# Attention, then two feed-forward layers in float32r on one Trainium2 core: the first layer's token parts moved to other distances, modulo 512 bytes, from the weights

## The chip, the core and the metric

The kernel runs on one core of one Trainium2 chip. The metric is the time of one execution on the device in microseconds (us). The core has TensorE (PE) for matmuls, VectorE (DVE), ScalarE (ACT) and GpSimd (POOL) for elementwise work, and SyncE (SP), whose queue issues nearly all DMAs here.

## The reference

Attention with 4 batches, 8 heads, 576 tokens and 64 columns a head, then two feed-forward layers over the 2304 tokens.

```python
scores = scale * np.matmul(q, k.transpose(0, 1, 3, 2))      # causal, softmax -> a
local = np.matmul(a, v)
mem_out = mem_ret / mem_norm                                # phi(q) times M_prev, over phi(q) times z_prev
attn_out = g * mem_out + (1 - g) * local
...
h = x @ w_in                                                # (2304 x 512) @ (512 x 2048)
x = softplus(h) @ w_out                                     # (2304 x 2048) @ (2048 x 512)
...
a, b = x @ w_a, x @ w_b                                     # (2304 x 512) @ (512 x 1536)
out = (a * b) @ w_out2                                      # (2304 x 1536) @ (1536 x 512)
```

## The kernel before, in words

**Stages.** Attention takes 16 units (a batch and a pair of heads each). Then come `h` (below: the first layer, matmul line L875), its product with `w_out` (the second layer, L1019), `a` and `b` together (the third, L875 again), and the last product (L1019 again). The 2304 tokens go in three groups of 768.

**One product.** Each layer multiplies blocks of two by two by Strassen's scheme, so seven products, numbered 1 to 7, stand for eight. For each, the token side is a sum or difference of blocks; so is the weight side. Each operand is split into two float32r parts, high and low ("h" and "l"), and three matmuls (h times h, h times l, l times h) replace one float32 matmul. A first-layer unit (one of eight blocks of `w_in`, one token group) is 7 products of 6 matmuls, so 42 matmuls of 384 columns; the first layer has 24 units, 1008 matmuls. In every one of them the weights are 128 columns of float32r (512 bytes a partition), loaded anew, and the token part is the operand that streams.

**Where the token parts lie.** `right_parts` makes, for a group, the 14 token parts (7 products, h and l) of 768 words each. They lie one after the other in SBUF from word X0 = 14848, X1 = 25600 and X2 = 36352 for the three groups (a word is 4 bytes; `in_order` sets the steps of 1536 words per product). The weights of the first layer lie from WL = 4096 in three buffers of 3584 words. All these are multiples of 128 words, so every token part starts at the same place modulo 512 bytes as every 128-column slice of the weights. In attention, `kh` and `kl` (the operand that streams in the score matmuls, L517) are taken in turn from two buffers of 576 words, and `qh`, `ql` (the weights there) from two of 512 words: for even units k lies at 0 bytes modulo 512 from q, for odd units at 256 bytes (576 words is 4.5 times 128; from the place of `kh`, word 30080, which is 235 times 128). The memory operand `mz` (L555) has two buffers, 264 words apart, and is read in slices of 65 words.

**Who sets the order.** The kernel records every operation with its operands (`Plan.add`), finds what each depends on, gives each a cost, and a list scheduler (`order`) writes one fixed order for each engine; a semaphore wait stands for each dependence. Inside one buffer, dependences are found word by word (`cells`). Between two buffers that overlap in SBUF, everything is taken together (`beside`): whoever writes the one waits for all earlier uses of the other, to the last.

```python
for o in self.over.get(name, ()):
    for wrote, read in self.state[o].values():
        yield from (n for n, _ in wrote)
        if not reads:
            yield from (n for n, _ in read)
```

**What else lies there.** During attention, X1 and the words behind it hold `kr0`, `kr1` (from word 25600), `qr`, `qh` and so on. After the first layer's last units, `Wide` (the second layer) puts its own buffers over the token parts: weights `w5` (product 5) at words 32768 to 36864, `w6` at 43008 to 47104, token tiles `t0` at 23552, `t1` at 36864 to 39936, `t2` at 12288, `t3` at 39936 to 43008. `left` loads one product's weights (`w5lf` and so on) and splits them (ACT makes h, DVE makes l, in two halves each); `sums` makes a product's token sums on DVE (a tile in two halves, `t00` and `t01`); `parts` makes a slice's h (ACT) and l (DVE) into four buffers `gx0` to `gx3` in turn. One product of the second layer is four such slices, 12 matmuls each, so 48 matmuls; the order of the products is 1, 2, 5, 6, 7, 3, 4.

Of the kernel before, what the change touches and what calls it, by code (L numbers as in the profile page):

```python
# [10 lines left out]
F32R = mybir.dt.float32r  # L11
# [11 lines left out]
HALF = 384  # L23
GT = 2 * HALF
# [299 lines left out]
def tile_kernel(ctx: ExitStack, tc: tile.TileContext, qt, kt, vt, mz, be, w_in, w_out, w_a, w_b, w_2, out):  # L324
    nc = tc.nc
    plan = Plan(tc)
    V, A, G, PE, SP = (
        Engine(plan, n, e) for n, e in (("DVE", nc.vector), ("ACT", nc.scalar), ("POOL", nc.gpsimd), ("PE", nc.tensor), ("SP", nc.sync))
    )
# [18 lines left out]
    def kept(shape, name):  # L348
        return plan.track(nc.dram_tensor(name, shape, F32, kind="Internal").ap())
# [3 lines left out]
    xs = [kept([128, KT, GT], f"xs{i}") for i in range(NG)]  # L353
# [10 lines left out]
    def put(name, words, *at, dtype=F32):  # L364

        tag = name + "_" * (name in where)
        where[name] = [plan.buffer(f"{tag}{i}", words, a, dtype) for i, a in enumerate(at)], [0]
# [27 lines left out]
    RAW, WL, X0, X1, X2, SUMS = 0, 4096, 14848, 25600, 36352, 49664  # L395
    put("raw", 2048, RAW, RAW + 2048)
    early, late, spare = space(X1), space(X2), space(SUMS)
    more = space(WL + 7168)
    for n, words in (("kr", S), ("qr", 640), ("qh", 512), ("ql", 512), ("kh", S), ("kl", S), ("ph", 640)):
        at = [early(words), early(words)] + [more(words)] * (n in ("kr", "qr"))  # L400
# [387 lines left out]
            sub(e, w[:, n:m, 1], d[:, n:m], f(w[:, n:m, 0]))  # L788
        return lambda n, h, k: w[:, SLOT[n], h, 128 * k : 128 * k + 128]

    def right_parts(src, at, step=2, e=V, raws=()):

        x = {
            n: [plan.buffer(f"x{n}{h}", GT, a + GT * i, F32R).rearrange("p (k t) -> p k t", k=2) for i, h in enumerate("hl")]
            for n, a in at.items()
        }
        t = []
        for k in range(2):
            r = (raws[k] if k < len(raws) else take("raw"))[:, 0 : 2 * GT].rearrange("p (k t) -> p k t", k=2)
            SP.dma_start(out=r, in_=src[:, 2 * k : 2 * k + 2])  # L800
            t.append(r)
        (b11, b12), (b21, b22) = ((r[:, :, 0:HALF], r[:, :, HALF:GT]) for r in t)

        def parts(n, b):
            for k in range(0, 2, step):
                u = slice(k, k + step)
                rnd(A, x[n][0][:, u], b[:, u])
                sub(e, x[n][1][:, u], b[:, u], f(x[n][0][:, u]))

        parts(1, b11)  # L810
        sub(e, b11, b12, b11)
        parts(5, b11)
        sub(e, b11, b22, b11)
        parts(6, b11)
        parts(2, b21)
        sub(e, b12, b22, b12)
        parts(7, b12)
        parts(3, b22)
        sub(e, b21, b21, b11)
        parts(4, b21)  # L820
        return x
# [5 lines left out]
    def in_order(at):  # L827
        return {n: at + 1536 * i for i, n in enumerate((1, 5, 6, 2, 7, 3, 4))}
# [70 lines left out]


    plan.stream = 1
    put("s", HALF, *(50688 + HALF * i for i in range(12)))
    put("plain", 1024, 47104, 48128)
    put("more", 768, 49152, 49920)
    at_w = [WL, WL + 3584, WL + 7168]
    W1, X = {}, {}
    X_AT = [in_order(X0), in_order(X1), in_order(X2)]

    def unit1(u, g):
        def out(i, j, s, bank):  # L910
# [13 lines left out]
    def prepare1(what):  # L924
        kind, n = what[0], int(what[1:] or 0)
        if kind == "t":
            put("s", HALF, *(53760 + HALF * i for i in range(5)), *(47104 + HALF * i for i in range(6)))
            return
        if kind == "w":
            W1[n] = left_parts(w_in[n], at_w[n % 3], G if n in FIRST else V)  # L930
        elif kind == "x":
            raws = [plan.buffer("third", 2048, 47104)] if n == 2 else []
            X[n] = right_parts(xs[n], X_AT[n], 2 - (n == 0), G if n == 0 else V, raws)
        else:
            spill_out()

# [305 lines left out]
```

## Time and profile before

| what | value |
|---|---|
| time, median of 3 runs | 920.23 us (919.73, 920.23, 921.40) |
| span of the profiled execution, first to last instruction | 918.2 us |
| PE busy | 905.9 us, 99% of the span, 6556 matmuls |
| DVE busy | 786.6 us, 86% |
| ACT busy | 564.9 us, 62% |
| POOL busy | 100.4 us, 11% |
| DMA | 172.16 MB, 187 GB/s on average |

The profiled execution has no device time of its own on the page. Its span is the time from its first instruction to its last, and it is 2.0 us under the median of the runs; what lies around it (start and end of the program) makes the difference. A matmul's duration in the trace (334 ns) overlaps the next one's, so its price is read from the distance between starts.

### The profile page before, as it was taken

How to read it: one execution, taken by the hardware profiler on the slowest of the kernel's cores; microseconds unless marked ns; L12 is line 12 of the kernel's file. 1: busy time of each engine (PE TensorE's matmuls, PEld its weight loads, DVE VectorE, ACT ScalarE, POOL GpSimd, SP SyncE). 2: the span in 40 equal slices, each digit the busy share in tenths (PEclk: the TensorE clock that was granted, in tenths of full speed). 3: DMA queues.
4: the chain of work that ended last, by engine and by line, in shares of the span. 5: the costliest groups of instructions: out<-in, count | busy, mean ns of one | idle time of the engine just before them, and what ended most of it. 6: DMA issues, size and time to landing. Idle time of an engine off the chain costs nothing.

```text
span 918.2 us, 17626 instructions
## 1 busy us (share of the span) xinstructions
PE 905.9 (99%) x6556; PEld 868.2 (95%) x6556; DVE 786.6 (86%) x1487; ACT 564.9 (62%) x1124; POOL 100.4 (11%) x140
## 2 busy tenths in 40 slices
PE   6999999999999999999999999999999999999998
PEld 4777778899999999999999999999999999999998
DVE  6999999789999658988599999999899666988683
ACT  7999999677677576744456655444444344655442
POOL 6445667100000000000000000000000000000000
PEclk9999999999999999999999999999999999999999
DMA  7656654468889889672720445455656156672701
GB/s 231 192 157 184 191 155 127 135 237 273 287 305 303 290 296 374 218 246 80 225 75 23 161 149 181 161 167 179 215 185 220 48 185 186 227 248 88 215 26 52
DMA packets 84870, 172.16 MB, mean 187 GB/s; under 512 B 8352, under 2 KB 60976, under 8 KB 82096
## 3 DMA queue, kind: packets, MB, share of 16 engines
q1 hardware_dynamic: 84352, 170.71, 56.9%
q8 instruction: 51, 0.84, 0.4%
q10 hardware_dynamic: 432, 0.33, 0.1%
q14 instruction: 35, 0.29, 0.1%
HBM read 110.90 MB, written 60.11 MB: 186 GB/s over the span
## 4 chain that ended last, share of the span: by engine, by line
PE 98%; DVE 1%; DMA 0%; issue 0%; ACT 0%; SPq 0%; DVEq 0%
PE bank L875 48%; PE bank L1019 33%; PE bank L627 4%; PE bank L597 4%; PE bank L517 4%; PE bank L555 1%; PE bank L668 1%; PE bank L647 1%; PE bank L614 1%; PE bank L635 1%; DVE eTrue L527 0%; DMA kr<-kt 0%; PE bank L570 0%; PE bank L653 0%; PE bank L615 0%
## 5 line engine op out<-in xcount | busy, mean ns | idle before, releaser
L346 DVE TENSOR_TENSOR s<-bank,s 128x384 f32<-128x384 f32 x216 | 117.9, 552 | 40.8 <-PE bank L875 31.5
L853 ACT ACTIVATE s<-bank 128x384 f32<-128x384 f32 x72 | 35.0, 486 | 81.2 <-PE bank L875 52.0
L343 DVE TENSOR_TENSOR t<-t,t 128x1536 f32<-128x1536 f32 (+1 forms) x48 | 74.5, 1552 | 0.4
L875 PE MATMUL bank<-x1h,w 128*128 128x384 f32 x240 | 70.7, 335 | 0.0
L875 PE MATMUL bank<-x5h,w 128*128 128x384 f32 x240 | 70.6, 334 | 0.0
L875 PE MATMUL bank<-x3h,w 128*128 128x384 f32 x240 | 70.5, 334 | 0.0
L875 PE MATMUL bank<-x7h,w 128*128 128x384 f32 x240 | 70.5, 334 | 0.0
L875 PE MATMUL bank<-x6h,w 128*128 128x384 f32 x240 | 70.5, 334 | 0.0
L875 PE MATMUL bank<-x2h,w 128*128 128x384 f32 x240 | 70.5, 334 | 0.0
L875 PE MATMUL bank<-x4h,w 128*128 128x384 f32 x240 | 70.5, 334 | 0.0
L336 ACT ACTIVATE w<-wf 128x256 fp32r<-128x256 f32 (+1 forms) x100 | 50.1, 501 | 19.4 <-DVE w L343 14.7
L911 ACT ACTIVATE s<-s 128x384 f32<-128x384 f32 x72 | 37.5, 523 | 32.9 <-DVE s L346 32.5
L850 ACT ACTIVATE s<-bank 128x384 f32<-128x384 f32 x72 | 34.9, 485 | 32.1 <-PE bank L875 16.6
L336 ACT ACTIVATE gx1h<-t 128x768 fp32r<-128x768 f32 x37 | 31.3, 847 | 34.4 <-PE bank L1019 33.1
L336 ACT ACTIVATE gx2h<-t 128x768 fp32r<-128x768 f32 x37 | 31.4, 847 | 34.2 <-PE bank L1019 31.8
L343 DVE TENSOR_TENSOR w<-wf,w 128x256 fp32r<-128x256 f32 (+1 forms) x90 | 47.3, 525 | 3.7 <-ACT w L336 3.2
L336 ACT ACTIVATE gx0h<-t 128x768 fp32r<-128x768 f32 x37 | 31.3, 846 | 30.4 <-PE bank L1019 28.9
L759 ACT ACTIVATE raw<-raw 128x512 f32<-128x512 f32 (+1 forms) x54 | 43.2, 802 | 9.0 <-DVE raw L758 8.6
L343 DVE TENSOR_TENSOR gx1l<-t,gx1h 128x768 fp32r<-128x768 f32 x37 | 35.3, 954 | 13.5 <-ACT gx1h L336 13.3
L343 DVE TENSOR_TENSOR gx0l<-t,gx0h 128x768 fp32r<-128x768 f32 x37 | 35.3, 954 | 12.8 <-ACT gx0h L336 12.5
L856 ACT ACTIVATE s<-bank 128x384 f32<-128x384 f32 x72 | 35.3, 490 | 17.1 <-PE bank L875 12.9
L336 ACT ACTIVATE gx3h<-t 128x768 fp32r<-128x768 f32 x36 | 30.4, 845 | 24.1 <-PE bank L1019 24.0
(340 smaller groups left out, 2982.1 us busy)
## 6 DMA issues: line engine op xcount, KB each, us to landing
gs<-s SPq DMA_DIRECT2D x96, 192.0 KB
t<-gs SPq DMA_DIRECT2D x24, 768.0 KB
us<-s SPq DMA_DIRECT2D x72, 192.0 KB
t<-us SPq DMA_DIRECT2D x12, 768.0 KB
raw<-w_out SPq DMA_DIRECT2D x8, 1024.0 KB
raw<-w_in SPq DMA_DIRECT2D x12, 512.0 KB
raw<-w_a SPq DMA_DIRECT2D x12, 512.0 KB
raw<-w_b SPq DMA_DIRECT2D x12, 512.0 KB
```

The costliest lines, as they stand in the source:

```text
L336: A.activation(out=o, in_=i, func=AF.Copy)
L343: eng.tensor_tensor(out=o, in0=a, in1=b, op=ALU.subtract)
L346: eng.tensor_tensor(out=o, in0=a, in1=b, op=ALU.add)
L517: PE.matmul(out=s[:, j, at : at + L], lhsT=a[r, qc], rhs=b[r, 0:L], start=t == 0, stop=t == 2, skip_group_check=True,)
L597: PE.transpose(out=s[:, 128 * n : 128 * n + 128], in_=Es[i, j][:, 128 * k : 128 * k + 128], identity=ident)
L627: PE.matmul(out=self.po[both[j], 128 * k :], lhsT=self.vr[:, k, 64 * j : 64 * j + 64], rhs=a, start=False, stop=k == 3, skip_group_check=True,
L759: A.activation(out=f(high), in_=f(high), func=AF.Identity, scale=REBIAS)
L853: A.activation(out=self.s5, in_=bank["c"], func=AF.Copy)
L856: A.activation(out=self.s2, in_=bank["b"], func=AF.Copy)
L875: PE.matmul(out=o, lhsT=w(n, a, k), rhs=x[n][c][:, k], start=start and k == t == 0, stop=k == 1 and t == 2, skip_group_check=True,)
L911: A.activation(out=s, in_=s if bank is None else bank, func=AF.Softplus)
L1019: PE.matmul(out=o, lhsT=self.w[n][a][:, u, 128 * m : 128 * m + 128], rhs=x[c][:, j], start=start and u == t == 0, stop=u == self.nu - 1 an ...
```

## The change

`right_parts` gets a further argument. With it, a group's 14 parts are no longer 14 buffers but slices of one buffer "xx_", and each slice is shifted: in the first group the i-th part by 8 times i words (0, 32, 64 up to 416 bytes), in the second group all by 116 words (464 bytes), in the third all by 192 words (256 bytes modulo 512). The buffers behind the third group (`plain`, `more`, `s`, `third`) move by 256 words. The third layer's calls have no such argument and stay as they are.

```diff
--- before.py
+++ after.py
@@ -788,12 +788,23 @@
             sub(e, w[:, n:m, 1], d[:, n:m], f(w[:, n:m, 0]))
         return lambda n, h, k: w[:, SLOT[n], h, 128 * k : 128 * k + 128]
 
-    def right_parts(src, at, step=2, e=V, raws=()):
-
-        x = {
-            n: [plan.buffer(f"x{n}{h}", GT, a + GT * i, F32R).rearrange("p (k t) -> p k t", k=2) for i, h in enumerate("hl")]
-            for n, a in at.items()
-        }
+    def right_parts(src, at, step=2, e=V, raws=(), whole=None):
+
+        if whole is None:
+            x = {
+                n: [plan.buffer(f"x{n}{h}", GT, a + GT * i, F32R).rearrange("p (k t) -> p k t", k=2) for i, h in enumerate("hl")]
+                for n, a in at.items()
+            }
+        else:
+            lo, words, shift = whole
+            buf = plan.buffer("xx_", words, lo, F32R)
+            first = min(at.values())
+            x = {}
+            for n, a in at.items():
+                x[n] = []
+                for i in range(2):
+                    o = a + GT * i + shift((a - first) // GT + i) - lo
+                    x[n].append(buf[:, o : o + GT].rearrange("p (k t) -> p k t", k=2))
         t = []
         for k in range(2):
             r = (raws[k] if k < len(raws) else take("raw"))[:, 0 : 2 * GT].rearrange("p (k t) -> p k t", k=2)
@@ -899,12 +910,14 @@
 
 
     plan.stream = 1
-    put("s", HALF, *(50688 + HALF * i for i in range(12)))
-    put("plain", 1024, 47104, 48128)
-    put("more", 768, 49152, 49920)
+    put("s", HALF, *(50944 + HALF * i for i in range(12)))
+    put("plain", 1024, 47360, 48384)
+    put("more", 768, 49408, 50176)
     at_w = [WL, WL + 3584, WL + 7168]
     W1, X = {}, {}
     X_AT = [in_order(X0), in_order(X1), in_order(X2)]
+    SHIFT = [lambda i: 8 * i, lambda i: 116, lambda i: 192]
+    MOVED_ = [[X0, 10864], [X1 + 112, 10760], [X2 + 120, 10824]]
 
     def unit1(u, g):
         def out(i, j, s, bank):
@@ -924,13 +937,13 @@
     def prepare1(what):
         kind, n = what[0], int(what[1:] or 0)
         if kind == "t":
-            put("s", HALF, *(53760 + HALF * i for i in range(5)), *(47104 + HALF * i for i in range(6)))
+            put("s", HALF, *(53760 + HALF * i for i in range(5)), *(47360 + HALF * i for i in range(6)))
             return
         if kind == "w":
             W1[n] = left_parts(w_in[n], at_w[n % 3], G if n in FIRST else V)
         elif kind == "x":
-            raws = [plan.buffer("third", 2048, 47104)] if n == 2 else []
-            X[n] = right_parts(xs[n], X_AT[n], 2 - (n == 0), G if n == 0 else V, raws)
+            raws = [plan.buffer("third", 2048, 47360)] if n == 2 else []
+            X[n] = right_parts(xs[n], X_AT[n], 2 - (n == 0), G if n == 0 else V, raws, (*MOVED_[n], SHIFT[n]))
         else:
             spill_out()
 
```

Since the parts of a group are now one buffer, which also reaches further (the first group's to word 25712, over the first 112 words of `kr0`), `beside` finds other dependences and the scheduler writes another order. Three places show it.

On POOL, around the scores of the last attention units, this stood before; `x2l`, `x6l`, `x7l` are low token parts of the first group, `w_191` is the second weight block of the first layer, `kr0` the raw keys that units 0, 3, 6 up to 15 use.

```order
L340 TENSOR_SCALAR kh1_75<-kr0_64 128x576
L343 TENSOR_TENSOR kl1_77<-kr0_64,kh1_75 128x576
L582 TENSOR_SCALAR ss1_132<-sm1_126 128x9
L343 TENSOR_TENSOR raw0_62<-raw1_63,raw0_62 128x2x384
L343 TENSOR_TENSOR ql1_73<-qr0_67,qh1_71 128x512
L343 TENSOR_TENSOR raw0_62<-raw1_63,raw0_62 128x2x384
L343 TENSOR_TENSOR x2l_200<-raw1_63,x2h_199 128x384 x2
L343 TENSOR_TENSOR x6l_198<-raw0_62,x6h_197 128x384
L343 TENSOR_TENSOR raw1_63<-raw1_63,raw0_62 128x2x384
L343 TENSOR_TENSOR x6l_198<-raw0_62,x6h_197 128x384
L343 TENSOR_TENSOR x7l_202<-raw0_62,x7h_201 128x384
```

The same place after the change, where `xx__193` is the first group's one buffer:

```order
L340 TENSOR_SCALAR kh1_75<-kr0_64 128x576
L343 TENSOR_TENSOR kl1_77<-kr0_64,kh1_75 128x576
L582 TENSOR_SCALAR ss1_132<-sm1_126 128x9
L343 TENSOR_TENSOR ql1_73<-qr0_67,qh1_71 128x512
L343 TENSOR_TENSOR w_191<-wf_192,w_191 128x256
L343 TENSOR_TENSOR w_191<-wf_192,w_191 128x2x256 x2
L343 TENSOR_TENSOR xx__193<-raw0_62,xx__193 128x384
L582 TENSOR_SCALAR ss0_131<-sm0_125 128x9
L582 TENSOR_SCALAR ss0_131<-sm0_125 128x1
L343 TENSOR_TENSOR xx__193<-raw0_62,xx__193 128x384
L343 TENSOR_TENSOR raw0_62<-raw0_62 128x2x384
```

All 14 low parts of the first group now stand behind the last use of `kr0`; before, the first of them (`x1l`) stood 27 rows ahead of it on POOL.

On SP, at the change from the first layer to the second, before; `t10` to `t31` are halves of the token tiles 1 to 3, `w5lf` and `w6lf` the weights of products 5 and 6, `gs` the output of the first layer on its way to memory:

```order
L996 DMA t01_174<-gs0 128x1536
L996 DMA t21_178<-gs0 128x1536
L983 DMA w5lf_159<-wod 128x2048
L996 DMA t10_175<-gs0 128x1536
L778 DMA wod<-more1_151 128x3x256
L996 DMA t11_176<-gs0 128x1536
L996 DMA t30_179<-gs0 128x1536
L912 DMA gs0<-s1_137 128x384
L912 DMA gs0<-s5_141 128x384
L983 DMA w6lf_162<-wod 128x2048
```

And after:

```order
L925 DMA gs2<-s_10_219 128x384
L925 DMA gs1<-s_2_211 128x384
L996 DMA w3lf_171<-wod 128x2048
L1009 DMA t10_175<-gs0 128x1536
L996 DMA w5lf_159<-wod 128x2048
L1009 DMA t11_176<-gs0 128x1536
L1009 DMA t30_179<-gs0 128x1536
L996 DMA w6lf_162<-wod 128x2048
L1009 DMA t31_180<-gs0 128x1536
L996 DMA w7lf_165<-wod 128x2048
```

The loads of `w5lf` and `t10` stood ahead of the last stores of `gs1` and `gs2`; now they stand behind them, with `w3lf` ahead of them, and the wait of `t10` is for TensorE (the last matmul that reads the third group's buffer).

On DVE, the same place in the program, the end of the first layer's last units and products 1 and 2 of the second; before:

```order
L346 TENSOR_TENSOR s_3_251<-bank,s_3_251 128x384
L343 TENSOR_TENSOR w5l_158<-w5lf_159,w5h_160 128x1024
L343 TENSOR_TENSOR t00_173<-t10_175,t00_173 128x1536
L343 TENSOR_TENSOR gx0l_182<-t20_177,gx0h_181 128x768
L343 TENSOR_TENSOR w5l_158<-w5lf_159,w5h_160 128x1024
L343 TENSOR_TENSOR gx1l_184<-t20_177,gx1h_183 128x768
L343 TENSOR_TENSOR t01_174<-t11_176,t01_174 128x1536
L343 TENSOR_TENSOR gx2l_186<-t21_178,gx2h_185 128x768
L343 TENSOR_TENSOR t10_175<-t30_179,t10_175 128x1536
L343 TENSOR_TENSOR gx3l_188<-t21_178,gx3h_187 128x768
L343 TENSOR_TENSOR gx0l_182<-t00_173,gx0h_181 128x768
L343 TENSOR_TENSOR gx1l_184<-t00_173,gx1h_183 128x768
```

After (the numbers behind buffer names count all buffers, so `s_3_251` and `s_3_212` are the same buffer):

```order
L343 TENSOR_TENSOR gx3l_188<-t01_174,gx3h_187 128x768
L343 TENSOR_TENSOR gx0l_182<-t20_177,gx0h_181 128x768
L343 TENSOR_TENSOR gx1l_184<-t20_177,gx1h_183 128x768
L343 TENSOR_TENSOR gx2l_186<-t21_178,gx2h_185 128x768
L343 TENSOR_TENSOR gx3l_188<-t21_178,gx3h_187 128x768
L343 TENSOR_TENSOR w3l_170<-w3lf_171,w3h_172 128x1024
L343 TENSOR_TENSOR t00_173<-t10_175,t00_173 128x1536
L343 TENSOR_TENSOR w3l_170<-w3lf_171,w3h_172 128x1024
L343 TENSOR_TENSOR gx0l_182<-t00_173,gx0h_181 128x768
L343 TENSOR_TENSOR gx1l_184<-t00_173,gx1h_183 128x768
L343 TENSOR_TENSOR w5l_158<-w5lf_159,w5h_160 128x1024
L346 TENSOR_TENSOR s_7_216<-bank,s_7_216 128x384
```

The low half of `w5` and the sums of product 5 (`t00<-t10`, `t01<-t11`) stood between the slices of product 2 (`gx0l<-t20` to `gx3l<-t21`); now they stand behind all four.

## Rows read from the trace of the kernel before

**Rows 1.** The page, parts 1 and 4: busy time; the chain by engine.

```profile
PE 905.9 (99%) x6556; PEld 868.2 (95%) x6556; DVE 786.6 (86%) x1487; ACT 564.9 (62%) x1124; POOL 100.4 (11%) x140
...
PE 98%; DVE 1%; DMA 0%; issue 0%; ACT 0%; SPq 0%; DVEq 0%
```

**Rows 2.** The chain in order of time (start us, us, what), the change of layers.

```profile
173.16 172.49 PE bank L875 x994
345.65 2.08 PE bank L1019 x12
347.73 1.04 PE bank L875 x6
348.77 147.68 PE bank L1019 x852
```

**Rows 3.** The same chain, attention: the scores of units 6, 9 and 10.

```profile
62.18 2.11 PE bank L517 x24
...
92.56 2.12 PE bank L517 x24
...
101.90 2.11 PE bank L517 x24
```

**Rows 4.** The same chain, attention: the memory products of units 4 and 8.

```profile
54.95 0.74 PE bank L555 x40
...
94.67 0.74 PE bank L555 x40
```

**Rows 5.** The same chain: last reads of kr0, first matmuls of the first layer.

```profile
147.61 1.13 PE bank L668 x16
...
167.96 1.51 PE bank L875 x8
```

**Rows 6.** POOL's timeline (start us, us, engine line op out<-in): the first group's parts.

```profile
144.67 1.98 POOL L343 TENSOR_TENSOR x2l<-raw,x2h 128x384 fp32r<-128x384 f32 x2
...
147.57 1.83 POOL L343 TENSOR_TENSOR raw<-raw,raw 128x768 f32<-128x768 f32 x1
...
159.21 1.98 POOL L343 TENSOR_TENSOR x4l<-raw,x4h 128x384 fp32r<-128x384 f32 x2
```

**Rows 7.** SP's timeline: issues at the change of layers.

```profile
337.36 0.32 SPq L983 DMA_DIRECT2D w5lf<-wod  x1
340.48 0.32 SPq L996 DMA_DIRECT2D t<-gs  x1
...
341.52 1.36 SPq L996 DMA_DIRECT2D t<-gs  x2
```

**Rows 8.** DVE's timeline there.

```profile
345.69 0.56 DVE L346 TENSOR_TENSOR s<-bank,s 128x384 f32<-128x384 f32 x1 [0.42 <-PE bank L875]
346.80 1.23 DVE L343 TENSOR_TENSOR w5l<-w5lf,w5h 128x1024 fp32r<-128x1024 f32 x1 [0.56 <-ACT w5h L336]
347.94 1.75 DVE L343 TENSOR_TENSOR t<-t,t 128x1536 f32<-128x1536 f32 x1
349.61 0.95 DVE L343 TENSOR_TENSOR gx0l<-t,gx0h 128x768 fp32r<-128x768 f32 x1
350.48 1.22 DVE L343 TENSOR_TENSOR w5l<-w5lf,w5h 128x1024 fp32r<-128x1024 f32 x1
...
356.85 0.95 DVE L343 TENSOR_TENSOR gx3l<-t,gx3h 128x768 fp32r<-128x768 f32 x1
...
373.80 0.95 DVE L343 TENSOR_TENSOR gx3l<-t,gx3h 128x768 fp32r<-128x768 f32 x1
```

**Rows 9.** ACT's timeline there.

```profile
355.05 0.85 ACT L336 ACTIVATE gx3h<-t 128x768 fp32r<-128x768 f32 x1 [1.23 <-PE bank L1019]
...
359.96 1.05 ACT L336 ACTIVATE w6h<-w6lf 128x1024 fp32r<-128x1024 f32 x1
```

**Rows 10.** Busy time of the engines in two stretches, clock, DMA share, GB/s.

```profile
346.00:363.30 17.30, 17.30 (x101) 17.30 (x101) 15.35 (x15) 10.32 (x13) 0.00 (x0) 1.00 1.02 376
363.30:380.00 16.70, 16.70 (x99) 16.70 (x98) 16.70 (x15) 12.76 (x18) 0.00 (x0) 1.00 0.54 191
```

## The prediction

> **What bounds the kernel now.** The page comes first: TensorE (PE) is busy for 99% of the span, and the chain that ended last is PE for 98% of it, so what makes PE's stream longer or lets it wait makes the time longer [rows 1]. Next the chain in order of time: from 173.16 us PE runs first-layer matmuls without a gap, 994 in 172.49 us, which is 173.5 ns each, and then second-layer ones, 852 in 147.68 us, 173.3 ns each [rows 2]. The granted clock there is 1.00, so the 2.4 GHz level [rows 10]; at one column a cycle 384 columns would take 160.0 ns, and each matmul takes 13.3 ns more. Two things can therefore move the time: that spacing, for the 1008 first-layer matmuls whose token parts get other places, and a wait that the new order puts into a stream that has none.
>
> The second of these has to be looked for where PE's suppliers have little to spare. Around the change of layers DVE is busy 15.35 of 17.30 us, then 16.70 of 16.70 [rows 10]: it has no reserve there, and only work that it did ahead keeps PE going.
>
> **The spacing.** What it does at other distances the trace can show only in attention. The scores of even units read their streamed operand at 0 bytes, modulo 512, from the weights, those of odd units at 256 bytes. Units 6, 9 and 10 take 2.11, 2.12 and 2.11 us for the same 24 matmuls [rows 3]. The memory products read `mz` at 32 bytes in unit 4 and at 0 in unit 8: 0.74 us both times [rows 4]. The first of these is the same data type with weights of the same 128 columns, though on half the rows; the second is plain float32, a weaker witness. So I take 0 for all three groups. The bounds: the 13.3 ns could vanish (1008 times 13.3 ns is 13.4 us off), or could double, if the excess is a collision that other places make worse (13.4 us on). The third group is at 256 bytes, which the scores show; without it 672 matmuls are left, 8.9 us either way.
>
> The Trainium skill, "TensorE: Matmul & The Clock Gate", section "Back-to-back issue gap", gives a warm matmul columns over 2.4 GHz plus 2.5 ns, which is 162.5 ns for 384 columns, where the rows show 173.3 [rows 2]. If the 10.8 ns between them came from the place of the operands and went away in all 1008 matmuls, by that rule the sum would be 10.9 us lower. The same page, section "Step-by-step: what each phase is for", says that PE reads streamed operand and weights through two independent ports, so that a weight load takes nothing from the running matmul; by that the place can't matter and the sum below stands. No run so far shows which.
>
> **The first layer's start.** The first group's buffer now lies over the start of `kr0`, so ACT's high parts and POOL's low parts wait for the last read of `kr0`, the tail scores of units 14 and 15, which end at 148.7 us [rows 5]. POOL then has 14 low parts at 0.98 us (1.98 for two less their overlap) and 4 differences at 1.8 us [rows 6], 21 us, and some short sums: it ends near 173 us. PE takes its first parts at 168 us [rows 5], in the order 1, 5, 6, 2, then 1 of the next unit, then 3, 7, each 6 matmuls or 1.04 us; POOL delivers part 1 by 153, 5 and 2 by 163, 6 by 169, 3 by 171 and 4 by 173. Part 6 is wanted at about 174, part 3 at about 177, part 4 at about 183. Every part is 5 us early or more: price 0. The cover is that POOL's 21 us end before PE's third part; each microsecond by which POOL is later than those 5 costs one. The second group's raw loads come some 12 us later, behind POOL's last reads of the raw buffers, and PE wants its part 1 at about 182 us, ten products after the start; loads of 0.8 MB and 2 DVE halves fit in these 10 us, with less to spare. I take 0 here as well, and 1 us as its upper bound.
>
> **The second layer's start.** This is where the term lies. Before, the loads of `w5lf`, `t10`, `t11` and `t30` were issued at 337.4 to 342.9 us [rows 7], since each overlapped only parts that had been read by then. Now all of them overlap the third group's one buffer, so they wait for its last matmul, which ends at 348.77 us [rows 2]. That is 11.4 us later for `w5lf`. Ahead of them on SP stands `w3lf`. At 376 GB/s [rows 10], `w3lf` (1.05 MB), `t10` (0.79), `w5lf` (1.05) and `t11` (0.79) take 9.8 us; with a part of `w3lf` moved before, `t10` is there at about 354, `w5lf` at 357, `t11` at 359.
>
> PE does not wait for them at once: products 1 and 2 still fill it to 348.77 + 84 x 0.1733 = 363.3 us. What is lost is DVE's work ahead. Between 346.80 and 356.85 us DVE made both halves of `w5l`, the two sums of product 5 and one sum of product 7, between the slices of product 2 [rows 8]. Spaced start to start these cost 1.14 us for a weight half, 1.67 for a sum and 0.87 for a slice's low part [rows 8], so 2 x 1.14 + 3 x 1.67 = 7.3 us. In the new order all of it, and `w3l` too, stands behind the last slice of product 2. That slice can't come sooner, since its buffer is freed by PE: its high part runs on ACT from 355.05 to 355.90 [rows 9], its low part on DVE to about 357.0, and then `w3l` needs ACT's high half (1.05 us, as `w6h` [rows 9]), so DVE starts at about 357.4.
>
> From there DVE's new order has, up to the last slice of product 6: 6 weight halves, 5 sums, 8 low parts and one addition (0.56 [rows 8]): 6.84 + 8.35 + 6.96 + 0.56 = 22.7 us, without a gap, so that slice starts to leave DVE at 380.1 and is with PE at 380.3. PE wants it after 36 + 48 + 48 + 36 = 168 matmuls from 348.77 us, at 377.9. Before, the same slice was ready at 374.75 [rows 8], 3.1 us early; now it is 2.4 us late. The waits fall on slices of products 5 and 6, the first on `w5l`. Product 7 needs one more weight half and a low part at once, with ACT's evacuations behind in line: I add 0.4 (0 to 0.8). After that DVE has its lead again, and PE, which had no idle time before [rows 10], gives nothing back.
>
> Sum: 0 + 0 + 2.4 + 0.4 = 2.8 us. The profiled execution's span of 918.2 becomes 921.0; the median of the runs is 2.0 above that span, which gives 920.2 + 2.8 = **923.0 us**. Lower bound of the term: 1.4 us, if DVE starts at 357.0, without the wait for ACT, and spends 0.05 us less on each of its 20 steps. Upper bound 4.3 us, if the loads move at half that rate: `t11` then lands near 366.3, some 1.5 us after DVE's queue comes to the sum that reads it. The other stages keep their instructions.
>
> A measurement of this kernel can tell about 0.2%, 1.8 us, from no change.
>
> **The rivals.**
>
> Distance matters and helps (the other side). The place is the streamed read against the load of the next weights: at 0 bytes they may meet on every matmul and cost the 13.3 ns. For it: that the spacing is more than the columns' 160.0 ns by the same amount everywhere. Against it: the scores at 256 bytes [rows 3]. With 10 ns saved on 672 matmuls the time is 923.0 - 6.7 = 916.3 us; with all of the 13.3 ns on 1008, 909.6. It outweighs the wait from 2.8 us over 672, 4.2 ns each, and shows as faster from 6.9 ns. The gap formula of the Trainium skill's page above would, by 10.8 ns on 1008, end at 912.1. Chance 0.10.
>
> Distance matters and hurts. The old places are all alike, and the new ones include 32-byte steps and 464 bytes, which no row of float32r shows. With 5 ns more on 672 matmuls the time is 926.4; doubled, 931.9. Chance 0.12.
>
> The wait is hidden after all. DVE catches up since its steps up to product 6 are fewer or start sooner than I count; 2.4 us out of 22.7 is not much. For it: 3.1 us of reserve before, and waits for PE between slices that the new order may use better. Against: DVE's steps are counted from the order, and none can be passed. Time 920.2 to 921.6. Chance 0.12.
>
> **How the numbers follow.** The forecast, spacing unchanged and DVE late, has 0.66 and its own range 921.6 to 924.5; of it 0.05 lies within 0.2% of before. Faster: 0.10. Same: 0.12 + 0.05 = 0.17. Slower: 0.61 + 0.12 = 0.73. For 8 in 10 the range leaves out the helpful distances (0.10), the hurtful ones beyond 4 us on top (0.08) and a little of the hidden case: 920.1 to 926.7 us.
>
> **What would show it.** Right: starts of first-layer matmuls 173 or 174 ns apart at each of the 16 places; PE waits of 2 to 3.5 us in all between 360 and 390 us, for DVE's `gx..l` and `w5l`, and none between 175 and 348; `w5lf` issued just after the last first-layer matmul; DVE without a gap from about 357 to 380. Wrong: spacings that differ between parts or groups; PE waiting for POOL or ACT near 175, or for a load rather than DVE in product 5; no waits at all at the second layer's start.

## The result and the profile after

The changed kernel takes 927.48 us (median of four runs, 926.7 to 927.6) beside 920.21 us before: a ratio of 1.0067 [1.0055, 1.0079]. A later comparison of the same two kernels gave 925.33 us (925.1 to 926.4) beside 921.14 us, 1.0050 [1.0038, 1.0062]. So it is slower by 0.4 to 0.8%; why the two differ is told below. The forecast was 923.0 us.

The profiled execution after has a span of 924.9 us (its time is 926.7), 6.7 us over the 918.2 before. The page after, parts 1 and 4, against [rows 1]: PE's share of the chain has gone from 98% to 93%, and DVE and DMA have come into it. (Of DMA's 2%, 7.49 us stand for the load `raw<-w_a`, which the chain puts ahead of a DVE slice at 376.51 us; DVE's timeline has 0.13 us of idle time in that stretch, so that is no wait.)

```profile
PE 911.2 (99%) x6556; PEld 870.9 (94%) x6556; DVE 786.2 (85%) x1487; ACT 565.6 (61%) x1124; POOL 99.7 (11%) x140
...
PE 93%; DVE 3%; DMA 2%; issue 1%; ACT 1%; POOL 0%; SPq 0%; POOLq 0%; DVEq 0%
```

The chain after, in order of time (start us, us, what), against [rows 2, 3]. L886 is the first and third layer's matmul, L1032 the second and last layer's.

```profile
63.70 2.11 PE bank L517 x24
...
174.31 174.81 PE bank L886 x999
349.12 2.08 PE bank L1032 x12
351.19 1.04 PE bank L886 x6
352.24 6.25 PE bank L1032 x36
...
528.34 261.18 PE bank L886 x1506
```

Taken from stage to stage, the 6.7 us are:

- up to the scores of unit 6: 63.70 against 62.18 [rows 3], **+1.5 us**;
- from there to the first second-layer matmul: 349.12 - 63.70 = 285.42 against 345.65 - 62.18 = 283.47 [rows 2, 3], +1.95 us. The first layer's matmuls account for most: 174.81 us for 999 is 175.0 ns each, against 172.49 for 994, 173.5 ns [rows 2]; 1.45 ns times 1008 is **+1.5 us**. The other **0.5 us** are attention's;
- second layer, from its first matmul to the third layer's row: 528.34 - 349.12 = 179.22 against 521.79 - 345.65 = 176.14 (345.65 is in [rows 2], 521.79 in the row below), **+3.1 us**;
- the rest of the span: 396.56 against 396.41 us, +0.15.

The third layer's row in the chain before:

```profile
521.79 261.04 PE bank L875 x1506
```

The first of these is a matter of the execution and not of the change. Two executions of the changed kernel, PE's timeline (start us, us, engine line op, out<-in, count; in brackets the idle time before): first the one above, then one of the later comparison.

```profile
10.89 2.50 PE L668 MATMUL bank<-kr,qr 64*64 64x288 f32 x16 [1.61 <-DVE mn L527]
```

```profile
10.77 1.50 PE L668 MATMUL bank<-kr,qr 64*64 64x288 f32 x16 [1.61 <-DVE mn L527]
```

The same 16 matmuls, after the same wait, take 2.50 or 1.50 us (single ones 737 or 453 ns). The long form shows up in executions of kernels with the old places too (three of the experiments below: unit 6's scores then start at 63.4 or 64.69 us instead of some 62.1), so it has to be taken out before executions are compared.

TensorE's clock is behind it. Each trace holds a record of the granted clock, and it begins, at 1.00 (the 2.4 GHz level), at 15.12 us in the first of these two executions and at 8.77 us in the second. Ahead of that there is no record (a view shows 1.00 there all the same), but the matmuls tell: in the kernel before, where it begins at 9.71 us, pairs of score matmuls of 512 columns stand 427 ns apart at 7.8 us and 232 ns at 14.0 us; in the first execution here they stand 426 ns apart at 7.8 us and 230 ns at 15.5 us, and pairs of 384 columns still stand 320 ns apart at 13.8 us, against 168 ns in the kernel before at 12.6 us. In all 14 traces kept, the record begins either at 8.65 to 9.71 us (8 traces: the 16 matmuls take 1.50 us, unit 6's scores start at 61.9 to 62.4 us), at 14.2 to 15.3 us (5 traces: 2.50 us, 63.4 to 63.7 us) or at 17.38 us (one: 2.50 us, 64.69 us). Every one of them starts its first scores near 5 us; why the clock rises sooner in one execution than in another is not shown.

In a comparison with 33 runs of the kernel before, these lie in three clumps, at 919.8 to 920.4, 921.0 to 921.6 and 922.1 to 922.5 us; in the first comparison three of its four runs fell near 920, while the changed kernel's profile had the late start and its other three runs, of which no trace was kept, were 0.7 to 0.9 us longer still. Without the start, 6.7 - 1.5 = 5.2 us belong to the change.

What the prediction named for the second layer's start can now be looked at. SP's issues there, against [rows 7]: `w5lf` goes out at 352.63 us instead of 337.36, right behind the first layer's last matmul (the six of L886 at 351.19 in the chain).

```profile
350.18 0.32 SPq L996 DMA_DIRECT2D w3lf<-wod  x1
352.27 0.32 SPq L1009 DMA_DIRECT2D t<-gs  x1
352.63 0.43 SPq L996 DMA_DIRECT2D w5lf<-wod  x1
```

DVE's timeline there, against [rows 8]. It makes the slices of product 2 with 1 to 2 us of idle time ahead of each, in which before it made `w5l` and the sums of product 5; those come from 361.86 us on, among slices and other weights and with next to no idle time.

```profile
352.11 0.96 DVE L343 TENSOR_TENSOR gx0l<-t,gx0h 128x768 fp32r<-128x768 f32 x1 [1.24 <-ACT gx0h L336]
...
360.72 1.23 DVE L343 TENSOR_TENSOR w3l<-w3lf,w3h 128x1024 fp32r<-128x1024 f32 x1 [0.37 <-ACT w3h L336]
361.86 1.75 DVE L343 TENSOR_TENSOR t<-t,t 128x1536 f32<-128x1536 f32 x1
...
366.40 1.22 DVE L343 TENSOR_TENSOR w5l<-w5lf,w5h 128x1024 fp32r<-128x1024 f32 x1
...
382.73 0.95 DVE L343 TENSOR_TENSOR gx3l<-t,gx3h 128x768 fp32r<-128x768 f32 x1
```

And PE's waits between 349 and 400 us (line, what it waited for: us in total, times, longest), with one row of its weight loads (PEld). None of them is on a load from memory: the matmuls wait for DVE's parts of weights and slices, and two weight loads for ACT to empty a bank. Before, there were no waits of PE here; it was busy throughout [rows 10].

```profile
PE bank L1032 <- DVE w5l L343: 0.5, 1, 0.5
PE bank L1032 <- DVE gx3l L343: 0.4, 2, 0.2
PE bank L1032 <- DVE gx2l L343: 0.3, 1, 0.3
...
PEld bank L1032 <- ACT s L867: 0.6, 2, 0.3
```

The rows of PE make 1.2 us. A matmul behind a wait also starts its successor late; by the starts in the trace, 15 steps between 367 and 388 us are longer than 186 ns, by 2.96 us together over 173.3 ns each, which is nearly all of the second layer's loss. Eleven of them, 2.41 us, are at products 5 and 6, most right behind a part of DVE's; the last four, 0.55 us, are at the start of product 7, where ACT's copies of banks (`s`, L867) are waited for.

### The profile page after: what moved, and what is told of

The parts are those of the page before. It is cut to its first block, busy times and chain, and to the rows that moved or that the text cites. A ratio compares the mean times of both kernels' runs of the same rounds, so it can differ in the third digit from the quotient of the medians.

```text
span 924.9 us, 17638 instructions
## 1 busy us (share of the span) xinstructions
PE 911.2 (99%) x6556; PEld 870.9 (94%) x6556; DVE 786.2 (85%) x1487; ACT 565.6 (61%) x1124; POOL 99.7 (11%) x140
## 4 chain that ended last, share of the span: by engine, by line
PE 93%; DVE 3%; DMA 2%; issue 1%; ACT 1%; POOL 0%; SPq 0%; POOLq 0%; DVEq 0%
PE bank L886 47%; PE bank L1032 31%; PE bank L517 4%; PE bank L597 3%; PE bank L627 3%; PE bank L555 1%; PE bank L668 1%; PE bank L647 1%; DMA raw<-w_a 1%; PE bank L614 1%; PE bank L635 1%; DVE eTrue L527 1%; DVE t L343 0%; DMA xs<-xx 0%; DMA kr<-kt 0%
## 5 line engine op out<-in xcount | busy, mean ns | idle before, releaser
L886 PE MATMUL bank<-xx__194,w 128*128 128x384 f32 x336 | 63.4, 338 | 0.0
L886 PE MATMUL bank<-xx__193,w 128*128 128x384 f32 x336 | 62.9, 337 | 0.0
L886 PE MATMUL bank<-xx__196,w 128*128 128x384 f32 x336 | 62.5, 335 | 0.0
L886 PEld LDWEIGHTS bank<-xx__194,w 128*128 128x128 f32 x336 | 59.4, 188 | 0.0
L886 PEld LDWEIGHTS bank<-xx__193,w 128*128 128x128 f32 x336 | 58.7, 188 | 0.3 <-ACT aT L603 0.2
L886 PEld LDWEIGHTS bank<-xx__196,w 128*128 128x128 f32 x336 | 58.9, 188 | 0.0
L336 ACT ACTIVATE gx2h<-t 128x768 fp32r<-128x768 f32 x37 | 31.4, 848 | 35.2 <-PE bank L1032 31.0
L343 DVE TENSOR_TENSOR gx0l<-t,gx0h 128x768 fp32r<-128x768 f32 x37 | 35.4, 956 | 14.6 <-ACT gx0h L336 14.2
L867 ACT ACTIVATE s<-bank 128x384 f32<-128x384 f32 x72 | 35.2, 489 | 16.9 <-PE bank L886 13.4
L758 DVE SCALAR_TENSOR_TENSOR raw<-raw 128x512 uint32<-128x512 uint32 (+1 forms) x54 | 44.4, 823 | 0.4
```

What stands on the lines that cost most here:

```text
L336: A.activation(out=o, in_=i, func=AF.Copy)
L343: eng.tensor_tensor(out=o, in0=a, in1=b, op=ALU.subtract)
L758: V.scalar_tensor_tensor(out=low, in0=high, scalar=0x80000000, in1=low, op0=ALU.bitwise_and, op1=ALU.bitwise_or)
L867: A.activation(out=self.s2, in_=bank["b"], func=AF.Copy)
L886: PE.matmul(out=o, lhsT=w(n, a, k), rhs=x[n][c][:, k], start=start and k == t == 0, stop=k == 1 and t == 2, skip_group_check=True,)
```

## The experiments

Two theories stood from the start. The first: the change costs two things that add, the places themselves (through the distance from one matmul's start to the next) and the one buffer per group (through what must wait for a whole group). The rival: it is all the one or all the other. Where spacings of single kernels are compared, this table has them: start to start of successive first-layer matmuls, mean over some 990 of them (the first 800 in the three "own buffers" kernels), without the gaps of over 200 ns, worked out from the starts in each trace.

```
kernel                        distance, bytes modulo 512     mean ns   single steps
before                        0                              173.34    173, 174
one_buffer_at_0               0                              173.33    172 to 175
parts_apart_at_0              0                              173.33    173, 174
all_moved_by_128              0 (weights moved too)          173.34    173, 174
parts_apart_at_256            256                            173.33    173, 174
own_buffers_at_128            128                            176.00    174 175 182 176 173, in turn
the change                    32 apart; 464; 256             174.79    167 to 186
own_buffers_same_places       32 apart; 464; 256             174.80    167 to 185
parts_apart_changed_places    32 apart; 448; 256             174.22    168 to 185
second_group_alone_at_464     0; 464; 0                      175.16    170 to 185
```

**One buffer per group, all at distance 0.** The order of all instructions on every engine is the changed kernel's; only the places are undone.

```diff
-    SHIFT = [lambda i: 8 * i, lambda i: 116, lambda i: 192]
-    MOVED_ = [[X0, 10864], [X1 + 112, 10760], [X2 + 120, 10824]]
+    SHIFT = [lambda i: 128] * 3
+    MOVED_ = [[X0, 10880], [X1 + 128, 10752], [X2 + 128, 10752]]
```

> The changed kernel with every part back at 0 bytes, modulo 512, from the weights (all three groups shifted by 128 words); one buffer per group stays, and so does each engine's order. Theory 1 (two causes: the spacing costs 1.5 us, the new order the rest): first-layer matmuls 173.3 ns apart again, the time 1.5 us under the changed kernel, 926.0 us; waits of about 3 us at the second layer's start stay. Theory 2 (only the order costs, and the spacing differs because other engines' traffic came to lie beside it): spacing and time as in the changed kernel, 174.8 ns and 927.5 us. Theory 3 (only the places cost): back to 920.2 us.

Measured: 924.8 us, 1.0045 [1.0032, 1.0058]. The chain:

```profile
62.19 2.11 PE bank L517 x24
...
172.80 173.38 PE bank L886 x999
346.18 2.08 PE bank L1032 x12
...
525.38 261.18 PE bank L886 x1506
```

999 matmuls take 173.38 us instead of 174.81: the spacing is back at its old value, and the places are worth 1.4 us. The second layer takes 525.38 - 346.18 = 179.20 us, as long as with the change: its 3.1 us are not the places'. Attention's 0.5 us have stayed as well (346.18 - 62.19 = 283.99 us, against 283.47 before). They are there by unit 15's scores: in the two chains these start 152.58 - 62.19 = 90.39 us behind unit 6's, against 152.10 - 62.18 = 89.92 before.

**Parts with dependences of their own inside one allocation**, at the change's places, at 0 and at 128. They were to keep the order of before and leave only the places. The edit gives each part a name of its own in the plan's book-keeping:

```diff
-            buf = plan.buffer("xx_", words, lo, F32R)
+            buf = tc.nc.alloc_sbuf_tensor_at("xx_", [128, words], F32R, offset=START + 4 * lo).ap()
...
-                    x[n].append(buf[:, o : o + GT].rearrange("p (k t) -> p k t", k=2))
+                    u = plan.slice(f"x{n}{i}{lo}", buf[:, o : o + GT], lo + o, GT)
+                    x[n].append(u.rearrange("p (k t) -> p k t", k=2))
```

> The changed kernel's places, with dependences kept for each part apart as in the kernel before, and attention's buffers moved up by 128 words so that the first group's parts reach over none of them. The order is all but that of the kernel before. Theory 1: the spacing is that of the changed kernel (174.8 ns on average, the second group at 176), no waits at the second layer's start: 920.2 + 1.5 = 921.7 us. Theory 2: spacing 173.3 ns, 920.2 us. Theory 3: 927.5 us.

> As the run with the changed kernel's places and dependences of each part apart, same order on every engine, but all parts at 0 bytes from the weights: the control. All theories: 173.3 ns between starts, and the time of the kernel before within 0.5 us, 920.2 us; whatever it differs by is what the move of attention's buffers and the few steps in other order cost.

> As the control, all parts of all groups at 128 bytes, modulo 512, from the weights, where the changed kernel's first group had its shortest spacing (171.3 ns on 32 matmuls). If the distance itself sets the spacing: 171.3 ns in all 1008, so 2.0 us less than the control, 918.2 us. If the spacing depends on the step from one part's place to the next one's (uniform places have no such step): 173.3 ns and the control's time.

Measured: 946.1, 944.8 and 946.5 us, ratios of 1.0274, 1.0256 and 1.0276. So they aren't the controls that they were to be: the one at distance 0 should have been at 920. Its chain at the change of layers shows why.

```profile
339.03 2.89 PE bank L903 x15
...
341.94 4.55 DMA w5lf<-wod
...
346.53 5.32 PE bank L903 x20
...
351.86 4.70 DMA t<-gs
```

Each late load waits for the last matmul that read the parts under it, and the next first-layer matmul waits for the load, although it reads another part: the plan now orders the work by parts, but by these rows the waits in the built program still go by the whole allocation. PE's granted clock falls with the stops, to 0.74 between 352 and 372 us. That is what one buffer costs where the order takes no account of it, some 24 us; the change's own order, which puts these loads behind the first layer, pays 3. What the three are good for is the table: up to that point they share one order, and the places alone give 173.3, 174.8 and 176.0 ns. For 128 bytes neither expectation (171.3 or 173.3 ns) came true: a distance that all parts share can cost by itself.

**Parts apart.** Separate buffers as before the change, moved to distance 0 (512 bytes up) and to the change's distances, the second group at 448 bytes, since buffers of their own start at multiples of 32. The two have the same order on every engine.

```diff
-            n: [plan.buffer(f"x{n}{h}", GT, a + GT * i, F32R).rearrange("p (k t) -> p k t", k=2) for i, h in enumerate("hl")]
+            n: [
+                plan.buffer(f"x{n}{h}", GT, a + GT * i + shift((a - first) // GT + i), F32R).rearrange("p (k t) -> p k t", k=2)
+                for i, h in enumerate("hl")
+            ]
...
+    SHIFT = [lambda i: 128] * 3
...
+    SHIFT = [lambda i: 8 * i, lambda i: 112, lambda i: 192]
```

> Every x part of the first layer is a buffer of its own again, as before the change, all of them 512 bytes higher up (distance 0), with the staging slots where the change puts them. It is the control of this job. Theory 1 (the change costs two things that add: the places, through the matmuls' start-to-start distance, and the one buffer per group, through what must wait for a whole group): neither is here, so within 0.2% of before (918.9 to 922.6 us beside 920.7), 173.3 ns per first-layer matmul, no wait of PE in the second layer. Rival (the shifted staging slots or the higher place cost something by themselves): 923 us or more.

> The control with the change's distances: 0, 32, ... 416 bytes in the first group, 448 in the second (464 can't be had for a buffer of its own), 256 in the third. The order of all engines is that of the control. Theory 1: 1008 matmuls x (174.8 - 173.3) ns = 1.5 us over the control, so some 922.2 us, with PE's second layer free of waits. Rival A (the places only cost where the parts lie in one buffer, or by way of the one buffer's waits): the control's time. Rival B (the places are most of the change's 7.3 us): 5 us or more over the control.

Measured: 921.69 us, 1.0005 [0.9997, 1.0014], and 922.32 us, 1.0011 [1.0002, 1.0020]. The chains, the control's first:

```profile
63.36 2.11 PE bank L517 x24
...
174.16 172.67 PE bank L879 x995
346.82 2.08 PE bank L1024 x12
...
522.98 261.18 PE bank L879 x1506
```

```profile
63.72 2.11 PE bank L517 x24
...
174.52 173.55 PE bank L879 x995
348.06 2.08 PE bank L1024 x12
...
524.23 261.18 PE bank L879 x1506
```

The places alone, with no shared buffer and no other order, cost 173.55 - 172.67 = 0.88 us. That is less than the 1.5 expected; rival A is out, and so is rival B. The second group's 448 in place of 464 bytes is the only difference in places from the change, which has another order too; but with the change's places under a third order (`own_buffers_same_places`) the mean is the change's 174.8 ns, so the order isn't what makes it less. The second layer is 176.2 us in both: nothing of its 3.1 us is left. By runs alone the 0.6 us between the two medians would prove nothing, since single runs spread over 2.5 us; the rows show it.

**Which buffer makes the loads late.** All at distance 0, with the shared buffer for the first two groups alone, then for the third alone.

```diff
-            X[n] = right_parts(xs[n], X_AT[n], 2 - (n == 0), G if n == 0 else V, raws, (*MOVED_[n], SHIFT[n]))
+            X[n] = right_parts(xs[n], X_AT[n], 2 - (n == 0), G if n == 0 else V, raws, (*MOVED_[n], SHIFT[n]) if n in (0, 1) else None)
```

> Distance 0 throughout; the first and the second group in one buffer each, the third group's parts in buffers of their own. Theory 1 with the second layer's start as the prediction has it, and the third group's buffer as what the late loads wait for: the wait at the second layer's start is gone, some 0.3 to 0.6 us over the control are left from the attention's end; 921.0 to 921.5 us. Rival (the second group's buffer, which lies where w5l goes, is what the loads wait for): 3 us over the control, as with all three in one buffer at distance 0.

> Distance 0; the third group alone in one buffer, the first and the second apart. If the third group's buffer alone makes the second layer late: 3 us over the control, 923.5 to 924 us. If it takes the first group's buffer as well (whose waits change what the loads of the second layer stand behind): under 1 us over the control, some 921.4 us, with waits of PE of at most 0.7 us near 380 us.

Measured: 921.97 us, 1.0010 [1.0002, 1.0019], and 922.3 us, 1.0008 [1.0000, 1.0017]. The chain with the third group apart:

```profile
63.37 2.11 PE bank L517 x24
...
174.00 173.36 PE bank L886 x999
347.36 2.08 PE bank L1032 x12
...
523.59 261.18 PE bank L886 x1506
```

With the third group apart, the second layer takes 176.23 us and PE waits for nothing there; SP issues `w5lf` at 342.57 us, 8 us before the first layer's end. So the third group's buffer is what the loads wait for, as predicted. Up to the second layer it takes 283.99 us, the same 0.5 more than before as `one_buffer_at_0`: attention's part comes from the first two groups' buffers. Which of their instructions cost it stays open: PE's waits in attention behind unit 6 are 0.2 us in all (on DVE's `aT`), against none before. One thing that moved there is POOL's work, in 130 to 150 us (busy us of PE, PEld, DVE, ACT, POOL, then clock, DMA share, GB/s), first with parts apart, then with one buffer at 0:

```profile
130.00:150.00 20.00, 20.00 (x285) 15.70 (x286) 18.35 (x61) 19.29 (x55) 14.95 (x17) 1.00 0.51 163
```

```profile
130.00:150.00 20.00, 20.00 (x287) 15.52 (x284) 19.07 (x64) 19.44 (x55) 7.05 (x11) 1.00 0.46 131
```

With the third group's buffer alone, the chain is:

```profile
172.87 172.67 PE bank L886 x995
345.53 2.08 PE bank L1032 x12
...
348.68 4.27 DMA t<-gs
...
522.67 261.18 PE bank L886 x1506
```

`w5lf` goes out at 349.05 us, as late against the first layer's end as with the change, and yet the second layer loses only 522.67 - 345.53 - 176.14 = 1.0 us. The other 2 us take the first two groups' buffers as well. DVE's order is what differs:

```profile
353.73 0.96 DVE L343 TENSOR_TENSOR gx2l<-t,gx2h 128x768 fp32r<-128x768 f32 x1 [1.12 <-ACT gx2h L336]
354.68 1.22 DVE L343 TENSOR_TENSOR w3l<-w3lf,w3h 128x1024 fp32r<-128x1024 f32 x1
355.83 0.95 DVE L343 TENSOR_TENSOR gx3l<-t,gx3h 128x768 fp32r<-128x768 f32 x1
```

Here DVE makes the first half of `w3l` ahead of the last slice of product 2, in time in which with the change it stands idle (1.07 us ahead of that slice, 0.37 behind it), and the addition that stands between product 5's steps with the change (0.46 us from start to start) is not among them. So the last slice of product 6 leaves DVE 29.4 us behind the first layer's end, with the change 31.4; the steps longer than 186 ns cost PE 0.4 us at product 6 and some 0.55 at product 7 as there. The new order's price thus is in part what stands ahead of what on DVE. `w3lf`, the load of that weight, also goes out earlier: 345.93 us here, 348.23 with all three in one buffer, with the first layer ending 0.65 us apart. Whether the order on DVE would do alone was not tried.

**One group moved.** One buffer per group, the change's order, and only the second group at its changed place.

```diff
+    SHIFT = [lambda i: 0, lambda i: 116, lambda i: 128]
+    MOVED_ = [[X0, 10864], [X1 + 112, 10760], [X2 + 128, 10752]]
```

> One buffer per group as in the change and its order on every engine; only the second group stands at its changed place (464 bytes), the first and the third at distance 0. If a place's price goes by its own distance alone: the second group's 336 matmuls keep the mean that they have in the change's trace (175.9 ns at the step into them), the others 173.3; over all 174.2, so 0.9 us over the kernel with all three at 0 and 0.6 us under the change. Rival (the price comes from steps between groups at different distances, which here stand at two steps of three): the matmuls next to the second group are off too, and the mean over all is 174.8 or more.

Measured: 927.1 us, 1.0069 [1.0057, 1.0082], and in the chain:

```profile
172.55 175.17 PE bank L886 x999
```

175.17 us: moving one group costs 1.8 us, more than moving all three (174.81). The rival's number is met, but its rule isn't quite: within runs of second-group matmuls, all at 464 bytes, the steps go 174, 179, 174, 179 for whole products, and 305 steps between two matmuls of the third group, all at distance 0, have a mean of 174.9. So a matmul's step doesn't go by its own place alone. The trace says how far the past reaches: the first seven steps into distance 0 behind a matmul at 464 bytes have means of 179, 170, 175, 178, 185, 176 and 182 ns, the same each time to 1 ns, and from the eighth on all 433 are 173 or 174. The change's trace has it too: of the third group's steps, all into 256 bytes, those into the first seven matmuls of a run have a mean of 175.3 ns (157 steps), the others 173.35 (178 steps).

**All parts at 256**, the control with `SHIFT = [lambda i: 192] * 3`.

> The control with the parts apart, all three groups at 256 bytes. If the price goes by a place's own distance: the third group's mean in the change, 174.3 ns, at all 1008 matmuls, 1.0 us over the control. Rival (a step between unlike distances is what costs): every step here is from 256 to 256, so 173.3 ns.

Measured: 920.08 us in one run, and:

```profile
172.93 172.67 PE bank L879 x995
```

To the hundredth the control's 172.67 us. 256 bytes by themselves cost nothing, and the third group's 174.3 ns in the change come from what ran just before; the theory that prices each matmul by its own distance alone falls.

**Everything moved.** The kernel before, with its whole memory 128 bytes on.

```diff
-START, CONST, WORDS = 6272, 1280, 55680
+START, CONST, WORDS = 6400, 1280, 55680
```

> The kernel before with its whole memory 128 bytes further on, weights and tokens alike, so that each matmul's distance is 0 and its places modulo 512 bytes are others. If the distance between the two decides: 173.3 ns as before. If the token part's own place decides: as with the tokens alone moved by 128 bytes, 176.0 ns, and 2.7 us in the first layer (and some 6.7 us over all 2520 such matmuls).

Measured: 922.49 us in one run, with a late start, and:

```profile
175.67 172.49 PE bank L875 x994
```

994 matmuls in 172.49 us, as in [rows 2], where tokens alone at 128 bytes give 176.0 ns. So of the two theories it is the distance between tokens and weights that acts, not where the tokens stand.

**The change once more**, for its spread.

> The changed kernel once more, in one job with before, for its spread. The kernel before and the controls have shown times 1.2 and 2.3 us apart by their starts alone (16 scores matmuls at 10.9 us of 453 or 737 ns). If the change's first comparison had such starts on one side only: the median's distance to before is 5 to 6 us here (5.2 by the stages), with single runs from 925.2 up. If the late start belongs to the change: 6.7 us or more again, and no run under 926.5.

Measured: 925.33 us beside 921.14, five runs from 925.1 to 926.4. Its chain:

```profile
62.36 2.11 PE bank L517 x24
...
173.11 174.81 PE bank L886 x999
347.91 2.08 PE bank L1032 x12
...
527.10 261.18 PE bank L886 x1506
```

The start is at 62.36 us, 0.2 from before, and all the rest is as in the first profile: 285.55 us to the second layer and 179.19 us in it. From profile to profile the change now costs 923.7 - 918.2 = 5.5 us, of which 0.2 are the start. The 4.2 us between these medians are less than the 5.2 of the stages; six of the runs of before here lie near 921.2 us, as a profile with a late start does (`parts_apart_at_0`, 921.33 us), but no trace of these six was kept.

## Why the prediction came out as it did

The side was right (slower by over 0.2%, given 0.73), and so was the largest term. The sum was too small, since two terms were put at 0 that cost 1.5 and 0.5 us: 2.8 us forecast, 5.2 us measured by stages, 7.3 us between the first medians. The median of the first comparison lies 0.8 us above the range, that of the second inside it.

**The second layer's start: right in cause and size.** Forecast 2.4 + 0.4 = 2.8 us, measured 3.1, of which the steps of PE show 2.41 at products 5 and 6 and 0.55 at product 7. The loads behind the third group's last matmul, DVE's lost work ahead, no wait on a load, the waits on `w5l` and the slices of products 5 and 6, and ACT's copies of banks behind them are all as written, so the size isn't luck. DVE ran from 360.7 instead of 357.4 us, about as much as the first layer itself ended later (352.24 against 348.77). What the working did not see is that the third group's buffer alone costs 1.0 us. It gave the late loads as the reason, but took its steps from DVE's new order, and that order, with all of `w3l` behind product 2's last slice, takes the other two buffers as well.

**The spacing: this step failed.** "So I take 0 for all three groups" measured 1.45 ns on 1008 matmuls, +1.5 us. It was the rival "distance matters and hurts", at a smaller price than its 5 ns on 672 (3.4 us). The step rested on attention's scores at 256 bytes, which are as quick as those at 0 [rows 3]. That row said the truth about 256: `parts_apart_at_256` shows no cost either. It couldn't be carried to places that change from part to part, nor to 464 bytes (nor to 128, by `own_buffers_at_128`). Which share each of the first group's distances has, and what 464 bytes in all groups would cost, was not tried. The bounds of 13.4 us either way were nine times as wide as what came. The other rival, a gain by leaving distance 0, is out for each set of places tried: none has a mean under 173.33 ns.

By the Trainium skill, "TensorE: Matmul & The Clock Gate", section "Step-by-step: what each phase is for", streamed operand and weights come through two independent ports, and by that, as the prediction read it, the place couldn't matter. The runs show 173.3 to 176.0 ns by the place alone with the order unchanged; the measurement decides.

**The first layer's start: 0 was too little.** It measured 0.5 us, within the stated upper bound of 1 us. As the working said, PE did not wait for POOL near 175 us. What it left out is attention: the 0.5 us are lost there, before unit 15's scores, and the new order places attention's instructions differently too. How that makes the 0.5 us stays open.

**The rest** of the program, taken as unchanged, measured +0.15 us.

**The base.** The forecast was added to a median of runs that, as the later 33 show, clump near 920, 921.3 and 922.3 us. The profiles tie such steps to the start of the execution. 1.5 us of the profiled pair's 6.7 came from there, and no step of the prediction spoke of it.

## What to carry to other kernels

Where tokens and weights of back-to-back matmuls stand at one common distance that is quick (0 or 256 bytes here), leave all of them there: the other and the mixed distances tried here lost 0.5 to 1.5% of the matmuls' time and none gained. Joining buffers to get at places was dearer here (3.6 us) than the places (1.5 us), since every load that lies over a part then waits for the last reader of the whole; look for the engine whose work ahead of time it takes away. And before a difference of 0.2% is explained, compare the first 20 us of both executions: here the time at which the clock rose moved the end by 1.5 us by itself.

## What the runs showed of the hardware

- A float32r matmul of 384 columns with fresh weights has a start-to-start distance of 173.3 ns with tokens at 0 or at 256 bytes modulo 512 from the weights, and 176.0 at 128 bytes, in a cycle of steps such as 174, 175, 182, 176, 173. At 464 bytes among others at 0 it goes 174, 179 in turn, and the first seven matmuls at distance 0 behind them go between 170 and 185 ns, with a mean of 177.7, before the 173.3 are back. Moving weights and tokens together changes nothing. No rule found here gives all of these; that it depends on the distance and on the last few matmuls before is as far as the runs go.
- TensorE starts each execution slowly, and the record of its granted clock, at 1.00 (2.4 GHz), begins between 8.65 and 17.38 us in executions of one and the same program or nearly so. Pairs of score matmuls of 512 columns stand 426 or 427 ns apart ahead of it and 230 or 232 ns behind it, so what runs ahead of it has about half the speed, which fits the 1.2 GHz level. Where it begins at 14.2 us or later, unit 6's scores come 1.2 to 2.5 us later than where it begins by 9.7 us, and so does the end. What sets the moment stays open.
